# Third stage's weight conversions on a 22-unit step through the second stage

## The chip, the cores and the metric

The kernel runs on one core of a Trainium2 chip. A core has five engines with queues of their own: TensorE (PE in the profile, its weight loads PEld) for matmuls, VectorE (DVE), ScalarE (ACT), GpSimd (POOL) and SyncE (SP), which here only issues DMAs. The metric is the device time of one execution in microseconds. Before the change it was 1767.12 us, the median of three runs (1766.98 to 1773.9).

## The reference

Three stages on 4608 tokens of 512 numbers: attention over pooled keys and values, a mixture of eight experts of which each token takes two, and a dense layer pair with a curved activation.

```python
x = _attn_ref(q, k, v)                              # 8 x 8 heads x 576 x 64, reshaped to (4608, 512)
# second stage: 8 experts, w1 (8, 512, 1024), w2 (8, 1024, 512), top two per token
noisy = x @ w_gate + np.log1p(np.exp(x @ w_noise)) * noise
for e in range(8):
    h = np.maximum(x[mask] @ w1[e], 0.0)
    out[mask] += top2_w[mask, k, None] * (h @ w2[e])
# third stage: w_in (512, 2048), w_out (2048, 512)
h = x @ w_in
return (h - np.tanh(h)) @ w_out
```

## The kernel before

Every matmul of the second and third stage is made of three 16-bit ones: each operand is split into a high and a low half, and high x high, high x low and low x high are added in fp32. So weights have to be prepared before use: their largest absolute value gives a power of two as scale, ScalarE writes the high half, VectorE the low half.

The second stage goes expert by expert. An expert has 1216 token slots in three groups of 512, 384 and 320, and a group has eight units, one per 128 columns of the hidden layer: 24 units an expert, numbered 0 to 23 here, 192 in all. A unit is: the first layer for this unit (`L1`, 12 matmuls, lines 356 to 358, result `ph`), its relu in two halves `hT` (ScalarE line 360, VectorE line 361), now and then one block of 128 tokens of the next group, gathered by GpSimd (line 315), split into halves `xp` (lines 341, 342) and transposed by a DMA (line 343), and then the second layer of the unit two before (`L2`, lines 378 to 385, result `py`). When a group is done `Y` scales its results and stores them (lines 402 to 410) and takes their squares. There are two buffers of `ph`, four of `py`, five of `hT`, one of `xp`.

Other work rides along, put into units by a table of jobs written at lines 552 to 590: `at((e, u), f)` puts `f` behind the matmuls of unit u of expert e, and jobs of a unit run in the order in which they were put there. The order of each engine's instructions follows from it, nothing is scheduled later. The jobs are:

- The next expert's weights, c1 (w1) and c2 (w2): `load` into `stage`, `amax` (VectorE, line 127, four pieces), `fin1` (a TensorE transpose of the column of maxima, line 170, and a reduction, line 173), `fin2` (a matmul that spreads the maximum, line 183, and the scale, lines 101 to 103), `split` (lines 154 and 159, four pieces, into `pair`).
- The third stage's weights, eight conversions `Conv`, 0 to 3 for the four quarters of w_in, 4 to 7 for those of w_out. Each is loaded in eight pieces of 256 KB into the two buffers of `raw`, and each piece is turned from the given form of numbers into fp32 in `qf` by six VectorE instructions (`conv`, lines 239 to 244). Behind the eighth come `stat` (VectorE's maximum, line 248, and for w_in seven GpSimd instructions for the sum of squares, lines 252 to 255), `fin1`, `fin2`, `norm` (a matmul over the sums, line 271), `split` (lines 290, 291, into `wi` or `wo`), and for w_in `combos` (four VectorE instructions, lines 277 to 280) and the splits of these, stored to `ws_d`.

Units 0 to 7 of expert 0 share the engines with the end of the router: it still has to make the lists `idx` of tokens per expert (lines 1442 to 1517), and is dealt out in steps: `run_jobs` gives it a turn, `gate(4)`, of up to four steps after every job, and there are further turns in a unit. At the end of unit 7's first layer it is run to its end, and the first gathers from `x_d` follow; their tokens are transposed on TensorE (line 333).

```python
def run_jobs(key, between):
    for f, a in jobs.pop(key, []):
        f(*a)
        between()
...
            run_jobs((groups[i][0], KF * groups[i][1] + f), lambda: u < KF and gate(4))
```

Of the kernel before, what the change touches and what calls it, by code (L numbers as in the profile page):

```python
# [10 lines left out]
F32 = mybir.dt.float32  # L11
F16 = mybir.dt.float16
BF16 = mybir.dt.bfloat16
I32 = mybir.dt.int32
# [23 lines left out]
def kernel(ctx, tc, q, k, v, w_gate, w_noise, noise, w1, w2, w_in, w_out, out):  # L38
# [54 lines left out]
    with ExitStack() as st:  # L93
        moe(nc, tc, st, V, z)
# [81 lines left out]
def both(g):  # L176
    for _ in g:
        pass
# [8 lines left out]
def moe(nc, tc, st, V, z):  # L187
    w_in, w_out, hold, idx, ps, W, gate, sums = (V[n] for n in ("w_in", "w_out", "hold", "idx", "ps", "W", "gate", "ws_d"))
    N, E, DM, FF, F2, NT = (V[n] for n in ("N", "E", "DM", "FF", "F2", "NT"))
    identf, ones1, onec, x_d, y_d, wi, wo, cin, wn2, outc = (  # L190
        V[n] for n in ("identf", "ones1", "onec", "x_d", "y_d", "wi", "wo", "cin", "wn2", "outc"))
    wk = st.enter_context(tc.tile_pool(name="m_wk", bufs=2))
# [3 lines left out]
    KD, KF = DM // 128, FF // 128  # L196
# [7 lines left out]
    for e in range(E):  # L204
        c = 0
# [5 lines left out]
    class Conv:  # L211
# [34 lines left out]
        def stat(self):  # L246
            self.m = wk.tile([128, 1], F32, name="cq")
            nc.vector.tensor_reduce(self.m, self.f, axis=AX.XY, op=OP.max, apply_absolute_value=True)
            if self.which == 0:
                s = self.s = wk.tile([128, 512], F32, name="qs", bufs=1)  # L250
                s2 = wk.tile([128, 512], F32, name="qs2", bufs=1)
                nc.gpsimd.tensor_mul(s, self.f[:, 0], self.f[:, 0])
                for m in range(1, 4):
                    nc.gpsimd.tensor_mul(s2, self.f[:, m], self.f[:, m])
                    nc.gpsimd.tensor_add(s, s, s2)
# [41 lines left out]
    def at(key, f, *a):  # L297
        jobs.setdefault(key, []).append((f, a))
# [255 lines left out]
    for e in range(E):  # L554
        if e + 1 < E:
            c1, c2 = PR[e + 1, 1], PR[e + 1, 2]
            d = 4 if e == 0 else 0
            for c in range(4):
                at((e, d + c), c1.load, [c])
            at((e, 7 + d), lambda c=c1: both(c.fin1()))  # L560
            at((e, 8 + d), lambda c=c1: both(c.fin2()))
            for c in range(4):
                at((e, 3 + d + c), c1.amax, c)
                at((e, (12 if d else 10) + c), c1.split, c)
                at((e, 18 + c // 2), c2.amax, c)
                at((e, 22 + c // 2), c2.split, c)
            at((e, 15 if d else 13), c2.load)
            at((e, 20), lambda c=c2: both(c.fin1()))
            at((e, 21), lambda c=c2: both(c.fin2()))
        cv = Conv(e // 4, e % 4)  # L570
        for j in range(8):
            u = (0, 1, 2, 3, 8, 10, 11, 13)[j] if e == 0 else j + 3 if e < 5 else (j + 2 if j < 6 else j + 4) if e + 1 < E else (j + 4 if j < 5 else j + 6)
            if j < 2 and e == 0:
                cv.load(j)
            elif j < 2:
                at((e, j + 2 * (e + 1 == E)), cv.load, j)
            at((e, u), cv.conv, j)
            if j + 2 < 8:
                at((e, u), cv.load, j + 2)
        at((e, 14), cv.stat)  # L580
        at((e, 15), cv.fin1)
        at((e, 16), cv.fin2)
        at((e, 16), cv.norm)
        for j in range(4):
            at((e, 20 + j // 2), cv.split, j)
            if cv.which == 0:
                if j == 0:
                    at((e + 1, 0), cv.combos)
                at((e + 1, 1 + j // 2), cv.split, j, True)

    def clear():
        zero = wk.tile([128, DM], F32, name="ys", bufs=3)
# [8 lines left out]
    for u in range(len(units) + LAG):  # L601
        if u < len(units):
            i, f = units[u]
# [3 lines left out]
            n = -(-groups[i + 1][3] // 128) if i + 1 < len(groups) else 0  # L607
# [1152 lines left out]
```

## Time and profile before

| | us |
|---|---|
| median of three runs | 1767.12 |
| profiled execution, whole | 1768.31 |
| its span in the profile | 1766.5 |
| TensorE busy in the span | 1724.0 |
| VectorE busy | 1285.0 |
| ScalarE busy | 922.6 |
| GpSimd busy | 277.0 |

The second stage lies from about 217 to 1045 us of the span. A timeline row gives the start, the length, the engine and line, the operation with what it writes and reads, its form and count, and in brackets the idle time of the engine before it with what ended it. Rows of neighbouring instructions of one kind may be merged, and lengths of matmuls overlap, since they are pipelined. A windows row gives a stretch, its length, each engine's busy time in it, and then the granted clock of TensorE as a share of 2.4 GHz.

### The profile page before, as it was taken

Reading aid. Unit: us, or ns where it says so; the run is one execution under the profiler, and the core shown is the slowest. Engines: PE = TensorE matmul, PEld = TensorE weight load, DVE = VectorE, ACT = ScalarE, POOL = GpSimd, SP = SyncE. Lnnn points to the kernel's source line nnn. Section 1 sums busy time; section 2 is a strip of 40 time slices with the busy share of each in tenths; the row PEclk is TensorE's granted clock in tenths of the full one; section 3 lists DMA queues with packets and bytes.
Section 4 is the critical chain, followed back from the end, with each engine's and each line's share of the span. In section 5 each row is a group of like instructions: output and inputs, shape, how many; then the busy total and the mean of one; then the engine's idle time right before and its main releaser. Section 6 shows DMA issues by size and latency. Waiting matters only on the chain. (4 is left out here: it accounts for less than half of the span.)

```text
span 1766.5 us, 28298 instructions
## 1 busy us (share of the span) xinstructions
PE 1724.0 (98%) x10456; PEld 1037.9 (59%) x10456; DVE 1285.0 (73%) x2566; ACT 922.6 (52%) x2229; POOL 277.0 (16%) x291
## 2 busy tenths in 40 slices
PE   8988899999999999999999999999999999999998
PEld 6988744455454545545454544666666666666664
DVE  7899867766667676666564558688787879788765
ACT  6887624434343443424243356466575757666554
POOL 3343113022030301101010111012020101110000
PEclk9999999999999999999999999999999999999999
DMA  9967334644755565554553435242231414131100
GB/s 249 274 174 199 97 101 133 164 129 138 223 135 158 139 146 149 140 134 123 155 144 81 125 94 147 55 90 69 46 93 39 88 27 96 36 79 53 33 25 26
DMA packets 264127, 203.44 MB, mean 115 GB/s; under 512 B 188129, under 2 KB 208609, under 8 KB 263969
## 3 DMA queue, kind: packets, MB, share of 16 engines
q1 hardware_dynamic: 251808, 162.16, 34.8%
q0 software_dynamic: 11904, 38.81, 8.5%
q8 instruction: 87, 1.43, 0.3%
q14 instruction: 72, 0.58, 0.1%
q10 hardware_dynamic: 256, 0.46, 0.1%
HBM read 121.82 MB, written 45.74 MB: 95 GB/s over the span
## 5 line engine op out<-in xcount | busy, mean ns | idle before, releaser
L360 ACT ACTIVATE hT<-ph 128x512 f16<-128x512 f32 (+2 forms) x192 | 96.9, 505 | 438.8 <-PE ph L358 427.9
L356 PE MATMUL ph<-xTp,pair 128*128 128x384 f16 (+2 forms) x736 | 245.5, 334 | 1.1 <-PEq L456 0.6
L357 PE MATMUL ph<-xTp,pair 128*128 128x384 f16 (+2 forms) x736 | 245.0, 333 | 1.6 <-issue 1.6
L358 PE MATMUL ph<-xTp,pair 128*128 128x384 f16 (+2 forms) x736 | 245.1, 333 | 0.0
L361 DVE SCALAR_TENSOR_TENSOR hT<-ph,hT 128x512 f16<-128x512 f32 (+2 forms) x192 | 110.8, 577 | 179.5 <-ACT hT L360 176.1
L1047 PE MATMUL py<-wo,gT 128*128 128x512 f16 x576 | 218.4, 379 | 1.0 <-issue 1.0
L1045 PE MATMUL py<-wo,gT 128*128 128x512 f16 x576 | 218.4, 379 | 0.1
L379 PE MATMUL py<-pair,hT 128*128 128x512 f16 x576 | 218.4, 379 | 0.0
L1046 PE MATMUL py<-wo,gT 128*128 128x512 f16 x576 | 218.4, 379 | 0.0
L380 PE MATMUL py<-pair,hT 128*128 128x512 f16 x576 | 218.4, 379 | 0.0
L378 PE MATMUL py<-pair,hT 128*128 128x512 f16 x576 | 218.4, 379 | 0.0
L904 PEld LDWEIGHTS <-wi 128*128 128x128 f16 x1536 | 150.2, 98 | 59.0 <-DMA y<-yp 0.9
L315 POOL DMA_INDIRECT xg<-x_d,idx x75 | 78.7, 1050 | 667.2 <-DVE xp L342 510.3
L718 POOL DMA_INDIRECT y<-y_d,ridx x64 | 78.8, 1232 | 519.0 <-DVE y L729 240.7
L356 PEld LDWEIGHTS <-pair 128*128 128x128 f16 x768 | 75.3, 98 | 76.3 <-issue 15.8
L357 PEld LDWEIGHTS <-pair 128*128 128x128 f16 x768 | 75.4, 98 | 58.7 <-issue 2.9
L358 PEld LDWEIGHTS <-pair 128*128 128x128 f16 x768 | 75.4, 98 | 57.0 <-issue 1.1
L1004 ACT ACTIVATE th<-th,bias 128x512 f32<-128x512 f32 x144 | 102.5, 711 | 3.3 <-DVE th L1002 1.6
L1005 DVE SCALAR_TENSOR_TENSOR th<-th,t 128x512 f32<-128x512 f32 x144 | 98.8, 686 | 1.4 <-ACT th L1004 1.4
L1001 DVE SCALAR_TENSOR_TENSOR t<-hb,cinf,hs 128x512 f32<-128x512 f32 x64 | 48.0, 750 | 70.8 <-ACT hs L1000 68.7
L994 DVE TENSOR_TENSOR gT<-th,gT 128x512 f16<-128x512 f32 x144 | 98.9, 687 | 0.2 <-ACT gT L993 0.2
L1047 PEld LDWEIGHTS <-gT 128*128 128x128 f16 x576 | 56.3, 98 | 69.3 <-issue 1.5
(317 smaller groups left out, 3429.3 us busy)
## 6 DMA issues: line engine op xcount, KB each, us to landing
stage<-in_moe_w SPq DMA_DIRECT2D x64, 512.0 KB
y_d<-ys SPq DMA_DIRECT2D x82, 256.0 KB
x_d<-xr SPq DMA_DIRECT2D x36, 256.0 KB
out<-o SPq DMA_DIRECT2D x36, 256.0 KB
qt<-in_q SPq DMA_DIRECT2D x32, 256.0 KB
raw<-in_moe_w_in SPq DMA_DIRECT2D x32, 256.0 KB
raw<-in_moe_w_out SPq DMA_DIRECT2D x32, 256.0 KB
kt<-in_k SPq DMA_DIRECT2D x7, 768.0 KB
```

The source lines that it names most:

```text
L356: nc.tensor.matmul(p[:, :nt], w[:, 0, m, s], x[:, 0, m, :nt], start=(m == 0), stop=False)
L357: nc.tensor.matmul(p[:, :nt], w[:, 0, m, s], x[:, 1, m, :nt], start=False, stop=False)
L358: nc.tensor.matmul(p[:, :nt], w[:, 1, m, s], x[:, 0, m, :nt], start=False, stop=(m == KD - 1))
L361: stt(h[:, 1, :nt], p[:, :nt], 0.0, h[:, 0, :nt], op0=OP.max, op1=OP.subtract)
L378: nc.tensor.matmul(p, h[:, 0, s], w[:, 0, f], start=(f == 0), stop=False)
L379: nc.tensor.matmul(p, h[:, 0, s], w[:, 1, f], start=False, stop=False)
L380: nc.tensor.matmul(p, h[:, 1, s], w[:, 0, f], start=False, stop=(f == KF - 1))
L904: nc.tensor.matmul(p, w[:, a, m], y[:, c, b, m], start=(start and m + x == 0), stop=(m == 1 and x == 2), skip_group_check=True)
L1004: nc.scalar.activation(q, q, AF.Square, bias=bias[:, 2:3], scale=SP5)
L1045: nc.tensor.matmul(p, g[:, 0, s], wo[:, 0, f], start=(f == 0), stop=False)
L1046: nc.tensor.matmul(p, g[:, 0, s], wo[:, 1, f], start=False, stop=False)
L1047: nc.tensor.matmul(p, g[:, 1, s], wo[:, 0, f], start=False, stop=(f == KF - 1))
```

## The change

The conversions are no longer one per expert. Conversion n (0 to 6) begins to load at unit 14 + 22n of the 192 and converts in the eight units of 17 + 22n to 29 + 22n that have most room by a table of VectorE work per unit (`room`); the maximum follows one unit after the last piece, then the first spread, the scale, and one unit behind it the sum and the splits. Conversion 7 stays in expert 7. By this the eight pieces of conversion 0 lie in units 20 and 21 of expert 0 and 0 to 5 of expert 1; of conversion 3 in units 11 to 21 of expert 3; of conversions 4, 5 and 6 up to units 21, 16 and 16 of experts 4, 5 and 6. The sums of squares are made in buffers of `raw` in place of `qs` and `qs2`. `fin1` and `fin2` of the next expert's w1 come one unit later in experts 1 to 6 (units 8 and 9).

```diff
@@ class Conv, stat
-                s = self.s = wk.tile([128, 512], F32, name="qs", bufs=1)
-                s2 = wk.tile([128, 512], F32, name="qs2", bufs=1)
+                s = self.s = wk.tile([128, 512], I32, name="raw", bufs=2).bitcast(F32)
+                s2 = wk.tile([128, 512], I32, name="raw", bufs=2).bitcast(F32)
@@ jobs
-            at((e, 7 + d), lambda c=c1: both(c.fin1()))
-            at((e, 8 + d), lambda c=c1: both(c.fin2()))
+            at((e, 7 + d + (e > 0)), lambda c=c1: both(c.fin1()))
+            at((e, 8 + d + (e > 0)), lambda c=c1: both(c.fin2()))
...
-        cv = Conv(e // 4, e % 4)
-        for j in range(8):
-            u = (0, 1, 2, 3, 8, 10, 11, 13)[j] if e == 0 else j + 3 if e < 5 else (j + 2 if j < 6 else j + 4) if e + 1 < E else (j + 4 if j < 5 else j + 6)
...
-            at((e, u), cv.conv, j)
...
-        at((e, 14), cv.stat)
-        at((e, 15), cv.fin1)
-        at((e, 16), cv.fin2)
-        at((e, 16), cv.norm)
-        for j in range(4):
-            at((e, 20 + j // 2), cv.split, j)
-            if cv.which == 0:
-                if j == 0:
-                    at((e + 1, 0), cv.combos)
-                at((e + 1, 1 + j // 2), cv.split, j, True)
+    size = [3 * KF * e + d for e in range(E) for d in range(3 * KF)]
+    room = [(5100, 3850, 3200)[u % (3 * KF) // KF] - (690, 580, 490)[u % (3 * KF) // KF] for u in size]
...
+    for u in range(0, 13):
+        room[u] = 0
+    step = 22
+    last = 3 * KF * (E - 1)
...
+    for n in range(8):
+        cv = Conv(n // 4, n % 4)
+        u0 = 16 + step * n if n < 7 else last + 4
+        us = sorted(sorted(range(u0 + 1, u0 + 14), key=lambda u: -room[u])[:8]) if n < 7 else             [last + d for d in (4, 5, 6, 7, 8, 11, 12, 13)]
+        for j, u in enumerate(us):
+            room[u] -= 1950
+            if j < 2:
+                unit(u0 - 2 + j, cv.load, j)
+            unit(u, cv.conv, j)
             if j + 2 < 8:
+                unit(u, cv.load, j + 2)
+        u0 = us[-1] - 13 if n < 7 else last
+        unit(u0 + 14, cv.stat)
+        unit(u0 + 15, cv.fin1)
+        unit(u0 + 16, cv.fin2)
+        unit(u0 + 17, cv.norm)
         for j in range(4):
+            unit((u0 + 17 if n < 7 else last + 20) + j // 2, cv.split, j)
+        if cv.which == 0:
+            unit(u0 + 19, cv.combos)
+            for j in range(4):
+                unit(u0 + 20 + j // 2, cv.split, j, True)
```

On TensorE, at the end of the router in expert 0, `l_row` and `l_col` are the tables from which the last lists come, `ph` is the first layer's result. Before, the last of its matmuls and what stands around them:

```order
L380 MATMUL py<-pair_2883,hT 128x512
L1513 LDWEIGHTS l_row
L1513 MATMUL pt<-l_col,l_row 128x160
...
L356 LDWEIGHTS pair_1481
L356 MATMUL ph<-x0T,pair_1481 128x512
```

The same place now (lines behind the table of jobs are 24 higher):

```order
L358 MATMUL ph<-x0T,pair_1481 128x512
L1537 LDWEIGHTS l_row
L1537 MATMUL pt<-l_col,l_row 128x160
...
L378 LDWEIGHTS hT
L378 MATMUL py<-pair_2883,hT 128x512
```

The matmuls stood between a second layer and the first layer of unit 7, and stand behind that first layer now.

On VectorE at the same place, `idx` being the lists and `hT` the relu's low half, before:

```order
L1508 TENSOR_TENSOR l_row<-slot,g_row 128x512
L361 SCALAR_TENSOR_TENSOR hT<-ph,hT 128x512
L1516 TENSOR_TENSOR idx<-pt,idx 128x8x10
L1517 TENSOR_TENSOR idx<-pt,idx 128x8x10
...
L1734 TENSOR_TENSOR coef<-dd,coef 128x36
L361 SCALAR_TENSOR_TENSOR hT<-ph,hT 128x512
L336 TENSOR_TENSOR xTp<-pt,xTp 128x4x128 x3
```

and now:

```order
L1532 TENSOR_TENSOR l_row<-slot,g_row 128x512
L361 SCALAR_TENSOR_TENSOR hT<-ph,hT 128x512
L1540 TENSOR_TENSOR idx<-pt,idx 128x8x10
L1541 TENSOR_TENSOR idx<-pt,idx 128x8x10
...
L1758 TENSOR_TENSOR coef<-dd,coef 128x36
L336 TENSOR_TENSOR xTp<-pt,xTp 128x4x128 x3
```

The hT of unit 7 stood behind the lists and the work on `coef`; now it is the one ahead of `idx`.

On VectorE in units 22 and 23 of expert 3, where `pair` is the next expert's w2 and `cq` the conversion's maximum, before:

```order
L361 SCALAR_TENSOR_TENSOR hT<-ph,hT 128x320
L159 SCALAR_TENSOR_TENSOR pair_6892<-stage,wsc,pair_6892 128x1024 x2
L361 SCALAR_TENSOR_TENSOR hT<-ph,hT 128x320
L159 SCALAR_TENSOR_TENSOR pair_6892<-stage,wsc,pair_6892 128x1024 x2
L361 SCALAR_TENSOR_TENSOR hT<-ph,hT 128x512
```

and now:

```order
L361 SCALAR_TENSOR_TENSOR hT<-ph,hT 128x320
L159 SCALAR_TENSOR_TENSOR pair_6859<-stage,wsc,pair_6859 128x1024 x2
L248 TENSOR_REDUCE cq<-qf 128x1
L361 SCALAR_TENSOR_TENSOR hT<-ph,hT 128x320
L159 SCALAR_TENSOR_TENSOR pair_6859<-stage,wsc,pair_6859 128x1024 x2
L173 TENSOR_REDUCE cx<-pt 1x1
L361 SCALAR_TENSOR_TENSOR hT<-ph,hT 128x512
```

The maximum over the whole quarter and the reduction that follows its transpose came in, behind the splits that were put into these units first.

## Rows read from the trace of the kernel before

**Rows 1.** Windows view by expert: stretch, length; engine busy (count); clock, DMA share, GB/s

```profile
431.80:535.40 103.60, 102.23 (x540) 50.96 (x539) 69.58 (x137) 41.60 (x76) 19.17 (x17) 1.00 0.62 171
...
738.20:839.20 101.00, 101.00 (x539) 50.98 (x538) 63.68 (x127) 38.84 (x73) 9.50 (x10) 1.00 0.52 137
```

**Rows 2.** Timeline, TensorE: start, length, line, operation, out<-in, form, count [idle <-releaser]

```profile
242.13 0.19 PE L1469 MATMUL pt<-mb,before 128*128 128x64 bf16 x1 [1.15 <-DVE mb L1465]
...
278.96 0.27 PE L170 MATMUL pt<-identf,cm 128*1 128x128 f32 x1 [1.78 <-DVE cm L130]
...
296.31 0.27 PE L170 MATMUL pt<-identf,cq 128*1 128x128 f32 x1 [1.10 <-DVE cq L248]
...
300.44 0.38 PE L183 MATMUL pt<-cx,onec 1*128 1x1 f32 x2 [0.29 <-DVE cx L173]
301.36 1.02 PE L271 MATMUL pt<-qs,onec 128*1 128x512 f32 x2 [0.55 <-POOL qs L255]
...
469.77 0.27 PE L170 MATMUL pt<-identf,cm 128*1 128x128 f32 x1 [0.85 <-DVE cm L130]
470.56 0.32 PE L356 MATMUL ph<-xTp,pair 128*128 128x384 f16 x1 [0.52 <-DMA xTp<-xp]
```

**Rows 3.** Timeline, VectorE, expert 0, unit 9.

```profile
274.31 0.75 DVE L408 TENSOR_SCALAR ys<-py,ysc 128x512 f32<-128x512 f32 x1 [1.24 <-DMA y_d<-ys]
```

**Rows 4.** Timeline, expert 0, unit 7, four engines.

```profile
253.38 0.44 PE L1513 MATMUL pt<-l_col,l_row 128*128 128x160 f16 x4
253.66 0.38 PE L356 MATMUL ph<-x0T,pair 128*128 128x512 f16 x1
253.86 0.24 DVE L1516 TENSOR_TENSOR idx<-pt,idx 128x80 int32<-128x80 f32 x1 [1.55 <-PE pt L1513]
...
255.29 0.94 POOL L315 DMA_INDIRECT xg<-x_d,idx  x1 [53.49 <-DVE few L1724]
...
256.25 0.38 PE L378 MATMUL py<-pair,hT 128*128 128x512 f16 x1
...
257.08 0.69 DVE L361 SCALAR_TENSOR_TENSOR hT<-ph,hT 128x512 f16<-128x512 f32 x1
...
258.84 0.60 PE L333 MATMUL pt<-identf,xg 128*128 128x128 f32 x4
```

**Rows 5.** DMA view, issues of gathers: out<-in, queue, operation, count, median us to landing.

```profile
xg<-x_d,idx POOLq DMA_INDIRECT x75, 5.0
...
y<-y_d,ridx POOLq DMA_INDIRECT x64, 3.3
```

**Rows 6.** Windows view, one conversion of expert 0, VectorE alone: stretch, length, busy (count).

```profile
270.90:272.50 1.60, 1.57 (x7) 1.00 1.11 200
```

**Rows 7.** Timeline, VectorE and TensorE, expert 5, units 17 and 18.

```profile
818.71 0.30 PE L356 MATMUL ph<-xTp,pair 128*128 128x320 f16 x1
818.89 0.49 DVE L361 SCALAR_TENSOR_TENSOR hT<-ph,hT 128x320 f16<-128x320 f32 x1 [2.50 <-ACT hT L360]
```

**Rows 8.** Timeline, VectorE and TensorE, end of expert 3.

```profile
631.11 2.48 DVE L159 SCALAR_TENSOR_TENSOR pair<-stage,wsc,pair 128x1024 f16<-128x1024 f32 x2 [0.55 <-ACT pair L154]
...
634.49 0.39 PE L356 MATMUL ph<-xTp,pair 128*128 128x512 f16 x1
```

**Rows 9.** Timeline, GpSimd and VectorE, expert 0, units 13 to 16.

```profile
290.93 1.05 POOL L252 TENSOR_TENSOR qs<-qf 128x512 f32<-128x512 f32 x1
290.97 3.08 DVE L159 SCALAR_TENSOR_TENSOR pair<-stage,wsc,pair 128x1024 f16<-128x1024 f32 x1
293.98 2.27 DVE L248 TENSOR_REDUCE cq<-qf 128x1 f32<-128x2048 f32 x1
...
298.13 2.06 DVE L159 SCALAR_TENSOR_TENSOR pair<-stage,wsc,pair 128x1024 f16<-128x1024 f32 x1
```

**Rows 10.** Timeline, TensorE, and windows view around 217.

```profile
217.16 0.61 PE L356 MATMUL ph<-x0T,pair 128*128 128x512 f16 x1 [2.29 <-DVE idx L1517]
...
215.20:222.00 6.80, 4.84 (x12) 1.80 (x13) 3.41 (x11) 0.83 (x1) 0.00 (x0) 0.50 0.35 117
```

More of the change, by code (lines that the diff above doesn't have):

```diff
@@ L569, in moe @@
             at((e, 21), lambda c=c2: both(c.fin2()))
-        cv = Conv(e // 4, e % 4)
-        for j in range(8):
-            u = (0, 1, 2, 3, 8, 10, 11, 13)[j] if e == 0 else j + 3 if e < 5 else (j + 2 if j < 6 else j + 4) if e + 1 < E else (j + 4 if j < 5 else j + 6)
[L573 to L576, printed above, removed]
-            at((e, u), cv.conv, j)
-            if j + 2 < 8:
-                at((e, u), cv.load, j + 2)
@@ new lines, in moe @@
+    for e in range(E):
+        o = 3 * KF * e
+        for d, w in ((9, 1200), (17, 600), (1, 1800 * (e > 0))):
+            room[o + d] -= w
+        for d in (0, 2, 5, 8, 10, 13, 15, 17, 19, 21):
+            room[o + d] -= 690
+        for c in range(4):
+            room[o + 3 + 4 * (e == 0) + c] -= 1200
+            room[o + (12 if e == 0 else 10) + c] -= 1300
+            room[o + 18 + c // 2] -= 1200
+            room[o + 22 + c // 2] -= 1300
+    for u in range(0, 13):
+        room[u] = 0
@@ new lines, in moe, with unit @@
+    step = 22
+    last = 3 * KF * (E - 1)
+    def unit(u, f, *a):
+        at(divmod(u, 3 * KF), f, *a)
+    for n in range(8):
[7 more added lines that the diff above has]
+            unit(u, cv.conv, j)
+            if j + 2 < 8:
+                unit(u, cv.load, j + 2)
[4 more added lines that the diff above has]
+        unit(u0 + 17, cv.norm)
+        for j in range(4):
+            unit((u0 + 17 if n < 7 else last + 20) + j // 2, cv.split, j)
[3 more added lines that the diff above has]
+                unit(u0 + 20 + j // 2, cv.split, j, True)
```

## The prediction

> **What bounds the kernel now.** I read the windows view first, by expert of the second stage [rows 1]. In expert 5 TensorE is busy 101.00 of 101.00 us at a granted clock of 1.00; in expert 2 it is busy 102.23 of 103.60 us. VectorE is busy 63.68 and 69.58 us in these two, so a third of its time is free. So the stage runs at TensorE's pace, and what the change moves (VectorE instructions, their loads, GpSimd's sums) shows in the time only where TensorE waits. All of it is done as often as before. What can be won is TensorE's idle time, what can be lost is a new wait of TensorE.
>
> Then TensorE's timeline for the waits themselves [rows 2]. Seven of them lie where the change reaches: 1.15 us for the router (L1469), 1.78 us for the first maximum of expert 1's weights (L170 <- cm), 1.10, 0.29 and 0.55 us for expert 0's conversion (L170 <- cq, L183, L271), 0.85 us again for a first maximum and 0.52 us for the transposed tokens behind it, both in expert 2. That is 6.24 us, 0.35% of the time: the change cannot gain much more than this, since the other experts stand at TensorE's pace.
>
> **Expert 0, the conversion gone from units 0 to 16.** The waits of 1.10, 0.29 and 0.55 us were for its maximum, its scale and its sum, which now come an expert later, with the sum's matmul a unit behind the scale: -1.94 us. The 1.78 us stay. The step waited for sits behind an eviction that VectorE could not write before a store had landed, until 274.31 [rows 3]; what follows it up to the maximum is the chain that TensorE waited for, and no conversion stands in it (one comes behind it, one had ended before 274.31).
>
> **The router behind units 0 to 7.** After each job of these units the router gets a turn of four steps. Ten jobs (four, two, two, two) leave units 0 to 3, so the router has ten turns less, and the order shows its pieces later: the last list matmuls, which stood ahead of the first layer of unit 7, stand behind it, and on VectorE the two idx additions come behind unit 7's hT. The 1.15 us wait goes, since four conversions no longer stand ahead of mb and its matmul comes a unit later. TensorE would reach the first token transpose at 258.84 - 1.15 = 257.69 [rows 4]. Ahead of it are a second layer (256.25 to 258.84, 2.59) and the list matmuls (253.38 to 253.66, 0.28), so unit 7's first layer ends at 254.82. Its hT starts 0.83 after that (257.08 against 256.25) at 255.65, and idx 0.6 later, at 256.25. From idx to the gather 1.43 (253.86 to 255.29): 257.68. The gather's landing has no row; it lay at most 3.55 us behind its start (TensorE took the tokens at 258.84 with no idle time) and not under the 0.94 of the instruction itself. Of the medians of the gathers, 5.0 us for those of x and 3.3 for those of y [rows 5], the first is past the 3.55; I take 3.3: 260.98. TensorE idles 3.3 us there and is 260.98 - 258.84 = 2.1 us later than before, the 1.15 us counted. Bounds: -1.15 (it lands in time) to +2.4.
>
> **First maximum a unit later, experts 1 to 6.** The matmul that waited 0.85 us in expert 2 has a whole unit (two layers of 2.59) more: -0.85. In that expert 0.52 us were for a token transpose that lay in the queue behind eleven stores of zeros and, ahead of these, two stores of sums that waited for the conversion's last step. The sums now go out at units 10 and 11, so the loads and transposes of units 2 to 5 go earlier: -0.52.
>
> **The conversions' new places.** Each still has six instructions, 1.6 us of VectorE [rows 6]. In units 0 to 12 of the experts they replace each other or the combinations and splits of the conversion before, a unit has 4.2 us on average (101 over 24) and VectorE 2.9 us of work in it (69.58 over 24), and TensorE needs a unit's hT only two units later, so that 1.6 us more in one unit are made up in the next: nothing. In unit 17 of experts 2 and 3 one stands between an eviction and the hT at 818.89, ahead of which VectorE waited 2.50 us for ScalarE (the same units in expert 5 [rows 7]): 1.6 in 2.5 us: nothing. The cover is gone there if anything above 0.9 us joins it. In experts 5 and 6 the maximum stands there instead: eviction to 816.39 (818.89 - 2.50), L248 with its 2.27 [rows 9] to 818.66, against TensorE's next unit at 818.71: 0 to 0.2 us each, taken as nothing.
>
> **The maximum in unit 22 of experts 3 and 4.** Here L248 comes behind the two conversions of the second weights, and its transpose on TensorE at the end of unit 23. In expert 3 before, the two conversions ran 631.11 to 633.59, TensorE began the next expert at 634.49 [rows 8]. L248 from 633.55 for 2.27 ends at 635.82, the transpose starts at 635.9: 1.4 us idle in expert 4. In expert 3 GpSimd's seven sums start with the last conversion too, just ahead of unit 22. Beside these sums in expert 0 such a conversion took 3.08 and 2.06 us [rows 9], against 1.24 each in rows 8: 1.8 and 0.8 more. I take the mean of the two for each of the two conversions, 2.6: 4.0 us idle in expert 3. Bounds: 1.4 (no collision) to 5.0 (1.8 twice). Behind the waiting transpose stands all of expert 4's first layer; behind L248 on VectorE hT of unit 23, two more conversions and the reduction, whose readers come one to two units later, so nothing is added.
> The page "SBUF — State Buffer" of the Trainium skill, section "Who interferes with whom", has a rule for this: a VectorE instruction with two SBUF inputs and a GpSimd instruction that reads SBUF exclude each other, the later one waits until the other has ended, and a reduction never collides. The 3.08 and 2.06 us agree, and so does L248 at 2.27 beside the sums. By the rule each of the two conversions waits out one or two of GpSimd's instructions of 1.05 us, 2.1 to 4.2 us in all in place of my 2.6.
>
> **Sums in the slots of raw, not in qs.** A following conversion's first load now waits for the sum's matmul. It comes 3 units behind it or more (unit 9 and 12 of expert 1, 7 and 10, 5 and 8, 1 and 6 in the next): over 10 us, nothing. Nor do I count a gain: no row shows a wait for qs but the 0.55 us counted.
>
> **Sum.** -1.94 - 0.85 - 0.52 = -3.3; +2.1 + 4.0 + 1.4 = +7.5; together +4.2 us. The profiled execution took 1768.31 us (span 1766.5), so its like would take 1772.5. The median of the runs is 1767.12, 1.2 us below it, and so I say 1771.3 us: 0.24% slower, which counts as no change, since a measurement of this kernel cannot tell differences below about 0.5% (8.8 us).
>
> **Rivals.** (a) The new waits stay covered: the gather lands before TensorE is there, and VectorE has the maximum in time. -3.3 - 1.15: 1762.7 us. For it: the landing is not shown, and VectorE is idle for 0.55 us just ahead of the two conversions [rows 8]. Against: the hT ahead of idx and the length of L248 leave no such room.
> (b) The clock. TensorE idled 2.29 us at 217.16 [rows 10], and over 215.2 to 222 its granted clock was 0.50, the lower of its two levels (1.2 GHz of 2.4). That costs half of 6.8, 3.4 us, a time. The new waits of 3.3 and 4.0 us are longer than that one. If the clock falls at both: 1771.3 + 6.8 = 1778.1, slower by 0.6%; at one, 1774.7. It decides from the point where one of the waits exceeds what the clock bears; against it, 1.78 us of idle left the clock at 1.00 [rows 1, 2].
> The page "TensorE: Matmul & The Clock Gate" of the Trainium skill, section "HAM oscillation — how this bites in real kernels", speaks for (b): gaps in TensorE's work put the clock back to half, and every burst behind one starts slow.
> (c) The queue. Raw loads now lie in units 12 to 17 of experts 1 to 4, beside the 2 MB of the second weights, and the token transposes share their queue. A transpose that lands late cost 0.52 us in expert 2; once in each of four experts is 2.1 us: 1773.4. Against: the transposes of unit 17 have seven units until they are read.
>
> **Chances and range.** Forecast 0.65, its own range 1767.5 to 1774.0 (expert 3 between 1.4 and 5.0, expert 0 down to 0). (a) 0.17, (b) 0.11 of which 0.04 at both places, (c) 0.07. To hold 8 in 10 the range goes to the middle of (a) and past (b) at one place: 1763 to 1776. Slower by over 0.5% (above 1775.9): (b) at both, and half of its other cases with the upper bounds of expert 0 and 3, 0.08. Faster by over 0.5% (below 1758.3) would need more than all waits of rows 2: 0.03. Within 0.5%: 0.89.
>
> **What would show it.** In the profile of the changed kernel: L1469 without idle time; the first transpose of gathered tokens with 2.5 to 3.7 us of it, released by the gather; L170 <- cq with about 4 us at the end of expert 3 and 1.4 at the end of expert 4, and none elsewhere; L159 of 2 to 3 us just ahead of the former; no wait for cm in expert 2, but still 1.5 to 1.8 us at the start of expert 0's second group; expert 5 and 6 at 100.9 to 101.3 us. It is wrong if the transposes at the ends of experts 3 and 4 do not wait, if the gather's transpose does not, or if the granted clock leaves 1.00 behind 222 us.

## The result, and the profile after

The changed kernel took 1784.6 us (median of six runs, 1780.27 to 1788.62) against 1769.57 us for the kernel before on the same chip (six runs, 1766.98 to 1773.9): a ratio of 1.0084, interval 1.0063 to 1.0105. That is slower by 0.84%, where 1771.3 us and a range of 1763 to 1776 us had been forecast. The profiled execution took 1780.27 us (span 1778.4), 11.96 us more than that of before, where the sum said 4.2.

First the windows view by expert, the columns as in [rows 1]: stretch, length, the engines' busy time, then TensorE's granted clock. These are experts 1 to 4 of the changed kernel.

```profile
330.00:436.10 106.10, 102.20 (x540) 50.95 (x539) 74.39 (x148) 41.48 (x76) 18.52 (x17) 1.00 0.57 145
436.10:538.10 102.00, 102.00 (x540) 50.99 (x539) 74.58 (x149) 41.33 (x76) 19.20 (x17) 1.00 0.60 178
538.10:646.90 108.80, 103.97 (x541) 51.41 (x540) 78.59 (x150) 41.47 (x76) 28.88 (x24) 0.98 0.52 137
646.90:751.00 104.10, 102.17 (x542) 50.97 (x540) 69.06 (x136) 41.50 (x77) 10.60 (x10) 1.00 0.53 143
```

Expert 2, which idled before, is full now: 102.00 us busy of 102.00. Experts 1, 3 and 4 are not. Expert 3 has a second mark, a clock of 0.98 and 2 us more of busy time for the same matmuls (the stretch takes in the start of expert 4). The waits themselves stand in TensorE's timeline, to be held against [rows 2]; in brackets the idle time and what ended it.

```profile
262.31 0.63 PE L333 MATMUL pt<-identf,xg 128*128 128x128 f32 x4 [3.29 <-DMA xg<-x_d,idx]
282.59 0.27 PE L170 MATMUL pt<-identf,cm 128*1 128x128 f32 x1 [1.91 <-DVE cm L130]
316.28 0.27 PE L170 MATMUL pt<-identf,cm 128*1 128x128 f32 x1 [0.64 <-DVE cm L130]
412.89 0.38 PE L378 MATMUL py<-pair,hT 128*128 128x512 f16 x1 [1.93 <-ACT ys L406]
422.38 0.27 PE L170 MATMUL pt<-identf,cm 128*1 128x128 f32 x1 [1.96 <-DVE cm L130]
627.67 0.27 PE L170 MATMUL pt<-identf,cm 128*1 128x128 f32 x1 [1.14 <-DVE cm L130]
642.36 0.27 PE L170 MATMUL pt<-identf,cq 128*1 128x128 f32 x1 [3.69 <-DVE cq L248]
735.80 0.27 PE L170 MATMUL pt<-identf,cm 128*1 128x128 f32 x1 [0.65 <-DVE cm L130]
748.08 0.27 PE L170 MATMUL pt<-identf,cq 128*1 128x128 f32 x1 [1.28 <-DVE cq L248]
```

The first, seventh and ninth row are the three waits that the prediction named: 3.29, 3.69 and 1.28 us, where it said 3.3, 4.0 and 1.4. The 1.78 us of expert 0 stayed (1.91). The waits of 1.15, 1.10, 0.29, 0.55, 0.85 and 0.52 us are gone. What it did not have are the rows at 316.28, 412.89, 422.38, 627.67 and 735.80. One of them has a forerunner in the kernel before that neither the prediction nor [rows 2] lists, in expert 1:

```profile
418.09 0.27 PE L170 MATMUL pt<-identf,cm 128*1 128x128 f32 x1 [0.50 <-DVE cm L130]
```

All five lie in the last group of an expert, where the second weights of the next one come in. In expert 1 two engines stand still there. ScalarE and VectorE, units 16 and 17:

```profile
409.04 0.29 DVE L239 TENSOR_SCALAR ca<-raw 128x256 int32<-128x256 int32 x1 [4.89 <-DMA raw<-in_moe_w_in]
411.63 0.63 ACT L341 ACTIVATE xp<-xg 128x512 f16<-128x512 f32 x1 [4.42 <-DMA xTp<-xp]
412.17 0.67 ACT L406 ACTIVATE ys<-py,ysc 128x512 f32<-128x512 f32 x1
412.90 0.74 DVE L408 TENSOR_SCALAR ys<-py,ysc 128x512 f32<-128x512 f32 x1
```

ScalarE wants to write the next tokens into `xp`, but the transpose of the ones before has not left it: there is one `xp`. VectorE wants to convert a piece of `raw` that has not landed. Behind the one stands the eviction L406, behind the other L408, TensorE needs their `py` back, and the maximum of the second weights (L127, L130) comes behind all that. SP's queue, seen as issues (start, length, line, operation, count), shows what stands ahead of both late transfers:

```profile
395.36 2.11 SPq L120 DMA_DIRECT2D stage<-in_moe_w  x4
397.57 1.20 SPq L293 DMA_DIRECT2D ws_d<-ys  x2
398.86 0.56 SPq L225 DMA_DIRECT2D raw<-in_moe_w_in  x1
401.42 2.05 SPq L343 DMA_TRANSPOSE xTp<-xp  x1
403.56 6.87 SPq L225 DMA_DIRECT2D raw<-in_moe_w_in  x2
```

The 2 MB of w2 are ahead, then two stores of sums (which the change moved here) and the raw load that VectorE waits for, then the transpose. Which of these the transpose waits for is not shown: of them only the raw load was moved in a run of its own (the second experiment below), and ScalarE still waited.

The clock is the last part. TensorE alone around the 3.69 us wait; the last three columns are clock, DMA share and GB/s:

```profile
640.00:642.30 2.30, 0.00 (x0) 1.00 0.00 0
642.30:645.00 2.70, 2.64 (x8) 0.56 0.00 0
645.00:647.00 2.00, 2.00 (x9) 0.74 0.00 0
647.00:649.00 2.00, 2.00 (x11) 1.00 0.00 0
```

The engine was idle, and when it came back it worked at the lower level (1.2 GHz) for some 3.4 us (an estimate from the two windows with a lower clock: twice 2.70 x 0.44 + 2.00 x 0.26). The first layer behind it took 4.43 us (642.47 to 646.90) instead of 2.59: 1.8 us.

### The profile page after: what moved, and what is told of

It is laid out like the page before. It is cut to its first block, busy times and chain, and to the rows that moved or that the text cites. A ratio compares the mean times of both kernels' runs of the same rounds, so it can differ in the third digit from the quotient of the medians.

```text
span 1778.4 us, 28325 instructions
## 1 busy us (share of the span) xinstructions
PE 1727.3 (97%) x10454; PEld 1041.3 (59%) x10456; DVE 1287.6 (72%) x2566; ACT 922.5 (52%) x2229; POOL 274.9 (15%) x291
```

## The experiments

Two questions: what makes the five unforeseen waits, and why the runs lie up to 8 us above the profiled one. All ratios are to the kernel before, run on the same chip; the changed kernel stands at 1.0084.

**Two buffers of xp.**

```diff
-        xp = wk.tile([128, 2, DM], F16, name="xp", bufs=1)
+        xp = wk.tile([128, 2, DM], F16, name="xp", bufs=2)
```

The rest of the edit makes room: the sum of a half block in `Y` stays in `ys` instead of `qs2`, and a scratch of expert 7 lies in `xp`.

> The changed kernel with two buffers xp instead of one (the scratch qs2 gives up its room: the half block of Y is summed in ys itself, one scratch of expert 7 lies in xp). Theory X: in experts 0, 1, 3 and 4 the transposes of gathered tokens now come behind raw loads in SP's queue, the one xp stays taken, ScalarE (L341) stands still ahead of the evictions L406, and the chain behind it is late. Then TensorE's waits of 1.93 (py <- ys L406) and 1.96 (cm) in expert 1 and of 1.14, 0.65 and 0.64 (cm) in experts 3, 4 and 0 fall to 0.5 in expert 1 and 0 to 0.2 elsewhere: 5.0 to 5.8 us less idle time, a ratio to the kernel before of 1.0084 - 0.003 = 1.005. Rival V: VectorE is simply too full in units 15 to 21, the cm waits stay within 0.3 us of what they were and only the 1.93 goes. Rival Q: the queue stays late, and the first layer waits for xTp instead, the time does not move (1.008).

Measured: 1779.78 us, ratio 1.0057 (1.0037 to 1.0077). The 1.93 us are gone, cm in experts 0, 3 and 4 fell to nothing, 0.30 and nothing, but in expert 1 the wait for cm is still there. TensorE and VectorE of this kernel:

```profile
416.33 0.27 PE L170 MATMUL pt<-identf,cm 128*1 128x128 f32 x1 [1.56 <-DVE cm L130]
...
404.23 0.30 DVE L239 TENSOR_SCALAR ca<-raw 128x256 int32<-128x256 int32 x1 [3.63 <-DMA raw<-in_moe_w_in]
```

ScalarE no longer stands, VectorE does: L408 comes behind the late `raw`. So theory X holds for three experts and for half of expert 1; rival V, a VectorE that is simply full, falls, since cm shrank in experts 0, 3 and 4 with VectorE's work unchanged.

**The first two raw loads two units earlier.**

```diff
-                unit(u0 - 2 + j, cv.load, j)
+                unit(u0 - 4 * (n < 7) - 2 * (n == 7) + j, cv.load, j)
```

> The changed kernel with the first two raw loads of conversions 0 to 6 two units earlier, which puts conversion 1's second load ahead of the 2 MB of w2 in SP's queue; xp stays single. Theory Q (the place in the queue): VectorE no longer stands 4.9 us for raw in unit 16 of expert 1, the transposes are not held up by it, and the waits of 1.93 and 1.96 us there fall to 0 and 0.5: 3.4 us, ratio 1.0065. Rival X (one xp): the transposes stay behind the 2 MB all the same, the 1.93 stays and only part of the 1.96 goes: 1.0075 to 1.0085. The waits of 0.64, 1.14 and 0.65 us (cm in experts 0, 3 and 4) lie behind single raw loads: by Q they shrink only where the second load moved.

Measured: 1784.96 us, ratio 1.0086 (1.0068 to 1.0104): nothing won. VectorE no longer waits for raw, ScalarE still waits for xp, and both of TensorE's waits stay:

```profile
411.35 0.63 ACT L341 ACTIVATE xp<-xg 128x512 f16<-128x512 f32 x1 [3.76 <-DMA xTp<-xp]
...
412.61 0.38 PE L378 MATMUL py<-pair,hT 128*128 128x512 f16 x1 [1.27 <-ACT ys L406]
422.11 0.27 PE L170 MATMUL pt<-identf,cm 128*1 128x128 f32 x1 [1.97 <-DVE cm L130]
```

The rival's outcome, and what was missing from both theories: there are two arms side by side, and the later one decides.

**Both edits.**

> The changed kernel with two xp and the loads two units earlier, without the later maximum and without the router's turns. Theory of two arms: in expert 1 ScalarE stands for the one xp and VectorE for raw that lies behind the 2 MB, and either alone makes Y late; each edit alone left the other (waits of 1.56 with two xp, of 1.27 and 1.97 with earlier loads). With both, TensorE waits neither at py nor at cm in experts 0, 1, 3 and 4 (0 to 0.3 us each); 3.3, 3.7 and 1.3 us (gather, two maxima) stay. Ratio 1.004 to 1.005, 0.001 to 0.002 below two xp alone (1.0057). Rival: the gain of the earlier loads in the full version needs the later maximum too; then 1.0055 and a wait of 1 us or more stays in expert 1 or 3.

Measured: 1775.86 us, ratio 1.0027 (1.0012 to 1.0041). In experts 0, 1 and 4 no such wait is left, in expert 3 one of 0.29 us; 3.21, 3.69 and 1.29 us stay as they should. That is lower than expected, with 1.004 just inside the interval. The earlier loads are worth nothing alone and about 0.3% once xp is double; the intervals of 1.0057 and 1.0027 overlap a little, so this size is not clear of noise, but the vanished waits in the profile are plain.

**The first maximum's spread put back.** The changed kernel with `7 + d` and `8 + d` again, run once.

> The changed kernel with the first maximum's transpose and spread put back to units 7 and 8 in experts 1 to 6. Theory: the shift alone took the 0.85 us wait for cm from expert 2; put back, TensorE waits again at unit 7 wherever VectorE is fuller than before, which by the new places (units 0 to 5 of expert 1, 0 to 3 of expert 2) is experts 1 and 2: 0.3 to 1 us each, nothing in 3 to 6. Rival: the conversions' new places took it, no such wait comes back.

Measured: 1794.99 us in its one run (1768.65 for the kernel before beside it). The theory falls: at unit 7 TensorE waits in none of experts 1 to 6. So the conversions' new places are enough to free expert 2 of its 0.85 us, and the shift was not needed for it. Of the 14.7 us by which this run lies above the profiled one of the changed kernel, some 7 go with the `xp` again, in expert 3 too this time, and the clock behind that; the rest is mostly a clock that fell behind the gathered tokens and in expert 7, about 3 us each:

```profile
626.86 0.63 ACT L341 ACTIVATE xp<-xg 128x512 f16<-128x512 f32 x1 [6.76 <-DMA xTp<-xp]
...
628.12 0.59 PE L378 MATMUL py<-pair,hT 128*128 128x512 f16 x1 [4.27 <-ACT ys L406]
```

In the other profiles with one `xp` and the new places there is no wait at this place, and the one in expert 1 lies between 0.96 us and this run's 3.38: these waits differ from run to run. One run cannot say whether the edit has a part in it.

**The spread's shift alone, in the kernel before,** run once.

> The kernel before with only the first maximum's transpose and spread one unit later in experts 1 to 6. Theory: the 0.85 us wait in expert 2 goes, the 0.52 us for the transposed tokens behind it stays or grows to 0.5 to 1.4 us (they are as late as before, and TensorE is 0.85 us sooner there), so little or nothing is won; all other waits as in the kernel before. Rival: both go, 1.4 us.

Measured: 1774.96 us in one run (1768.65 for the kernel before beside it). The 0.85 us are gone here too, and the tokens behind them are waited for longer:

```profile
474.97 0.32 PE L356 MATMUL ph<-xTp,pair 128*128 128x384 f16 x1 [1.56 <-DVE ca L241]
```

1.56 us in place of 0.85 and 0.52: the shift by itself wins nothing there. (The row names `ca`, which this matmul does not read; the bracket is inferred, and of what it reads only `xTp` is as late.) One run cannot say what the shift costs in the whole; this one was slower in places that the shift does not touch, up to the second stage and by falls of the clock in experts 0 and 7.

**The maximum of conversions 3 and 4 three units later.**

```diff
-        u0 = us[-1] - 13 if n < 7 else last
+        u0 = us[-1] - 13 + 3 * (n in (3, 4)) if n < 7 else last
```

> The changed kernel with the maximum of conversions 3 and 4 and all behind it three units later (unit 1 of the next expert in place of unit 22). Theory: the waits L170 <- cq of 3.69 us (end of expert 3) and 1.28 us (end of expert 4) go, and with the first of them the stretch at half clock behind it (1.8 us): 5 to 6.8 us less in a profile, ratio 1.0045 to 1.0055, and a smaller spread between runs if the clock fell there in the slower ones too. Rival: the maximum of 2.27 us is as late in its new place, with the seven sums beside unit 1 to 3, and TensorE waits there or at the next expert's own first maximum (1 to 3 us): ratio 1.007 to 1.009.

Measured: 1777.11 us, ratio 1.0039 (1.0028 to 1.0050). Neither wait is there, and none has come in their place at the start of experts 4 and 5. The gain is at the upper end of what was expected or above it, 5.0 us of idle time and 1.8 us of clock behind it, against 7.5 us by the medians.

**GpSimd's sums two units later, the maximum where it is.**

```diff
+        unit(u0 + 14 + 2 * (n == 3), cv.sums)
-        unit(u0 + 17, cv.norm)
+        unit(u0 + 17 + (n == 3), cv.norm)
```

> The changed kernel with GpSimd's seven sums of conversion 3 two units later than its maximum (unit 0 of expert 4) and the matmul over them one unit later. Theory: of the 3.69 us wait at the end of expert 3 the part from contention goes (two conversions at 3.86 instead of 2.48 us, and 1.9 us in the last piece's six instructions): 0.6 to 1.5 us stay, as at the end of expert 4 (1.28), and the clock does not fall behind it: 2.2 to 3.1 plus 1.8, 4 to 5 us less, ratio 1.0055 to 1.006. Rival: the place behind the two conversions is the whole cause, GpSimd being beside the point: the wait stays above 3 us, ratio 1.008.

Measured: 1779.85 us, ratio 1.0058 (1.0040 to 1.0075). Here is the contention, VectorE and GpSimd of the changed kernel, ahead of the 3.69 us wait:

```profile
632.49 1.24 DVE L239 TENSOR_SCALAR ca<-raw 128x256 int32<-128x256 int32 x1
...
634.70 1.22 DVE L244 SCALAR_TENSOR_TENSOR qf<-ca,cb 128x256 int32<-128x256 int32 x1
...
636.24 3.86 DVE L159 SCALAR_TENSOR_TENSOR pair<-stage,wsc,pair 128x1024 f16<-128x1024 f32 x2
640.03 2.27 DVE L248 TENSOR_REDUCE cq<-qf 128x1 f32<-128x2048 f32 x1
...
632.52 1.05 POOL L252 TENSOR_TENSOR raw<-qf 128x512 f32<-128x512 f32 x1
634.60 1.04 POOL L254 TENSOR_TENSOR raw<-qf 128x512 f32<-128x512 f32 x1 [1.03 <-PE ph L358]
...
637.12 1.90 POOL L254 TENSOR_TENSOR raw<-qf 128x512 f32<-128x512 f32 x1
639.10 2.13 POOL L255 TENSOR_TENSOR raw<-raw 128x512 f32<-128x512 f32 x1
```

and with the sums moved away, VectorE and TensorE:

```profile
633.86 0.28 DVE L239 TENSOR_SCALAR ca<-raw 128x256 int32<-128x256 int32 x1
...
635.12 0.42 DVE L244 SCALAR_TENSOR_TENSOR qf<-ca,cb 128x256 int32<-128x256 int32 x1
...
636.59 2.48 DVE L159 SCALAR_TENSOR_TENSOR pair<-stage,wsc,pair 128x1024 f16<-128x1024 f32 x2 [0.55 <-ACT pair L154]
638.99 2.28 DVE L248 TENSOR_REDUCE cq<-qf 128x1 f32<-128x2048 f32 x1
...
641.32 0.27 PE L170 MATMUL pt<-identf,cq 128*1 128x128 f32 x1 [1.29 <-DVE cq L248]
```

3.69 us are 1.29 of place and 2.40 of contention, and behind 1.29 us the clock stays. The two conversions L159 give 1.38 of the 2.40 (3.86 against 2.48); the rest comes from the last piece ahead of them (L239 and L244 among its six instructions), less the 0.55 us of idle time that it uses up. The reduction L248 takes the same beside GpSimd (2.27) as without it (2.28).

**Work in the waits.** 13 and 24 matmuls that nobody reads, written into a free `pt` ahead of the two long waits:

```diff
+    def fill(e, i, n, k):
+        p = psum([128, 512])
+        for _ in range(k):
+            nc.tensor.matmul(p[:, :n], W[e, 1].pair[:, 0, 0, 0:128], XTP[i][:, 0, 0, :n], start=True, stop=True)
```

> The changed kernel with matmuls nobody reads put in front of the two long waits: 13 of 128x512 (2.8 us) ahead of the first transposes of gathered tokens in expert 0, 24 of 128x320 (3.3 us) ahead of the transpose of conversion 3's maximum. The waits stay as long, TensorE only works in them. Theory C (the clock): in the three profiles so far that have the 3.69 us wait the granted clock fell behind it (1.8 us lost each time), behind the 3.3 us wait in one of three (2.8 us). Filled, the clock stays at 1.00 from 222 us to the end of expert 4: 2.5 to 4 us less in the median, ratio 1.006 to 1.007 against 1.0084, and runs that differ less. Rival: the slower runs have another cause, the ratio stays at 1.0075 to 1.009.

Measured: 1777.85 us, ratio 1.0052 (1.0034 to 1.0070). TensorE is let go as late as before, and the windows at the end of expert 3 (the matmuls lie at 639.33, the wait's rest of 0.33 us at 643.10) read:

```profile
640.00:643.00 3.00, 2.76 (x21) 1.00 0.00 0
643.00:645.70 2.70, 2.60 (x13) 1.00 0.00 0
```

No work was taken away and some was added, and the kernel is faster by 0.3%, 5 to 6 us (the intervals just overlap). Over all profiles of these kernels, the clock fell behind the 3.7 us wait in six of six, behind the 3.2 to 3.4 us wait in five of seven (not in the changed kernel's own), behind waits of 1.9 to 2.1 us inside the stage twice (1.97 and 2.03), never behind 1.3 us. For example in the kernel with the later sums, around its 3.27 us wait in expert 0:

```profile
258.00:260.40 2.40, 0.00 (x0) 0.84 0.56 135
260.40:264.00 3.60, 3.55 (x11) 0.50 0.55 154
264.00:266.00 2.00, 2.00 (x6) 0.50 0.21 86
266.00:270.00 4.00, 4.00 (x23) 0.94 0.22 62
```

What such a fall costs there can be read from the first token transpose to the next wait for cm: 21.33 us in this kernel (260.45 to 283.59, its 1.81 us of idle time taken off), 18.37 in the changed kernel, whose clock stayed (262.31 to 282.59, less 1.91): 2.96 us.

**The router's turns.** Ten empty jobs in units 0 to 3 of expert 0:

```diff
+    for u in (0, 0, 0, 0, 1, 1, 2, 2, 3, 3):
+        unit(u, lambda: None)
```

> The changed kernel with ten empty jobs in units 0 to 3 of expert 0 (four, two, two, two), so that the router gets its turns back; all else as it is. Theory: the last list matmuls stand ahead of unit 7's first layer again, the gather starts earlier, and TensorE's wait of 3.29 us at the first transposes of gathered tokens falls to 0 to 1.2 us (the kernel before had none there, but 1.15 us at the router's matmul of mb, which should not come back since no conversions stand ahead of it): 2.1 to 3.3 us less, ratio 1.0066 to 1.0072. If in the slower runs the clock fell behind that wait, another 1 to 2 us in the median: down to 1.0055. Rival: the gather's own 3.5 us are what counts and the wait stays above 2 us: 1.008.

Measured: 1778.98 us, ratio 1.0052 (1.0035 to 1.0069). No wait is left at the tokens, nor at the router:

```profile
257.13 0.60 PE L333 MATMUL pt<-identf,xg 128*128 128x128 f32 x4
```

The gain is slightly above what was expected (5.6 us by the medians against 3.3 us of idle time), which fits a clock that in most runs fell with the wait; only profiled runs show it.

**The three edits together** (two xp, later maximum, turns).

> The three edits together on the changed kernel. If the named waits are the whole loss and are independent, 5.4 (xp) + 6.8 (maximum) + 2.7 (turns) = 14.9 us go against the median of 1784.6: 1769.7, ratio 1.000, and since waits of 0.3 to 1.9 us that the kernel before had in experts 0 and 2 are gone too, down to 0.998. With a ratio above 1.003 something else in the change costs time (the sums in raw, the loads' new places). The mean granted clock should be 0.995 as in the kernel before, not 0.989 to 0.992.

Measured: 1767.52 us, ratio 0.9987 (0.9972 to 1.0002), clock 0.995. So no loss shows beyond the named waits. In expert 1 cm still waits 2.62 us, by the theory of the two arms the second one.

**The three and the earlier loads.**

> The version with two xp, the later maximum and the router's turns (0.9987 in its run), now with the first two raw loads two units earlier. If the place in the queue is what is left in expert 1, its waits of 0.77, 0.40 and 2.62 us fall to 0.5 together, and the 0.59 in expert 3 to 0: 3.3 to 3.9 us less, ratio 0.9965 to 0.997, faster than the kernel before. If the raw loads only push something else (transposes, the gathers' block), 0.998 to 1.000.

Measured: 1764.78 us, ratio 0.9967 (0.9954 to 0.9980): faster than both kernels, if by less than the 0.5% that was set as clear. Experts 1, 2 and 4:

```profile
324.70:426.60 101.90, 101.90 (x541) 51.06 (x540) 74.42 (x148) 41.38 (x77) 18.52 (x17) 1.00 0.57 151
426.60:528.60 102.00, 102.00 (x541) 50.99 (x540) 74.56 (x149) 41.32 (x77) 19.19 (x17) 1.00 0.62 179
...
630.80:732.80 102.00, 102.00 (x541) 50.99 (x540) 70.30 (x136) 41.24 (x77) 17.75 (x17) 1.00 0.55 146
```

From the second group of expert 0 to the end of expert 6 no wait above 0.25 us is left but the 1.77 us behind the store [rows 3].

## Why the prediction was wrong

By its own steps, in the profiled execution (us; a gain is negative):

| step | forecast | measured |
|---|---|---|
| expert 0's conversion | -1.94 | -1.94 |
| router and gather | +2.1 | -1.15 + 3.29 = +2.14 |
| expert 2, both waits | -1.37 | -1.37 |
| end of expert 3 | +4.0 | +3.69 |
| end of expert 4 | +1.4 | +1.28 |
| new places: expert 1 | 0 | 1.93 + (1.96 - 0.50) = +3.39 |
| new places: cm in experts 0, 3, 4 | 0 | 0.64 + 1.14 + 0.65 = +2.43 |
| clock behind the 3.69 us | 0 (rival b) | 4.43 - 2.59 = +1.84 |
| sum | +4.2 | +11.5 |

All of these lie in experts 0 to 4. The profiled runs differ by 11.96 us, but not all of that is the change: some 1.4 us had arisen by 222 us, since the granted clock was 0.50 from 113.6 to 120.4 us, in the first stage, where it was 1.00 in the kernel before. The change does not touch that stage, and in some profiles of the same kernel with another edit (two xp, earlier loads, later sums) this fall is missing. Behind expert 6 the changed kernel takes back 1.1 us.

- **Right:** the five steps that were worked out as chains of instructions, each within 0.3 us. The router's turns and the maximum behind the two conversions were the true costs that the order showed, and the runs with turns and with the later maximum took them away. The gather's chain held link by link, though the 3.3 us to its landing was a choice and not a row (TensorE took the tokens 3.46 us behind the gather's start, 258.85 to 262.31). The maximum in experts 5 and 6 cost nothing here; it cost 0.76 us in expert 5 of the kernel with turns and 1.22 in expert 6 of the one with earlier loads alone.
- **Right by luck: the size of the contention,** 2.40 us measured, 2.6 taken. The prediction put all of it on the two conversions; they lost 1.4 (3.86 against 2.48), and the piece ahead of them, which it had at nothing, made up the rest. The rule of the Trainium skill ("SBUF — State Buffer", "Who interferes with whom") was worked out, as an estimate, to 2.1 to 4.2 for the two conversions; the trace lies below that. That the Trainium skill counts tensor_scalar there among those that can take the shared port agrees with L239 (1.24 us against 0.28).
- **Wrong: the term of nothing for "The conversions' new places", and rival (c) with it.** The step compared VectorE's time with VectorE's room. It took `raw` as landed, which in unit 16 of expert 1 it was not, for 4.89 us. And rival (c) was put aside because "the transposes of unit 17 have seven units until they are read". That counts the reader of `xTp`; the transpose also sets free the only `xp`, and ScalarE, which evicts `py`, stands in front of that one unit later. This made +5.8 us, and the prediction's bounds for the step held none of it. Three runs settle it: xp alone, loads alone, both.
- **Wrong: the clock as a rival of its own, at 0.11.** Its places were right, its size too large (1.84 us behind the 3.69 us wait, 2.96 behind the other where it fell, instead of 3.4), and it was a follower of the two waits that the forecast itself had: behind 3.69 us it fell each time. It should have been a term. The measure that the prediction took for it, 2.29 us with a fall and 1.78 without, was misread. These are the rows ahead of that wait, in the kernel before and in the changed one:

```profile
214.00 0.87 PE L1513 MATMUL pt<-l_col,l_row 128*128 128x160 f16 x10 [1.94 <-DVE l_row L1508]
215.85 1.44 PE L1537 MATMUL pt<-l_col,l_row 128*128 128x160 f16 x10 [1.93 <-DVE l_row L1532]
```

In the kernel before the wait of 2.29 us ran from 214.87 to 217.16, and the clock was at 0.50 already from 215.2 on [rows 10]. In the changed kernel it was 0.51 over 215.85 to 222.70, so that it fell behind the wait of 1.93 us, with one of 1.72 still to come. So the kernel before did not show that 1.8 to 2.3 us is where a fall begins; the runs show only how often it came behind each wait. The Trainium skill's rule that gaps put the clock back ("TensorE: Matmul & The Clock Gate", "HAM oscillation — how this bites in real kernels") agrees with the 3.69 us every time, with the 3.3 us five times in seven.

- **The median above the profile.** Its profiled run was the fastest of six. In the other five the mean granted clock is 0.989 to 0.991 against 0.992; at half speed 0.001 of 1780 us is 3.6 us long and loses 1.8, so by this estimate 2 to 5 us of the 3 to 8 between these runs and the profiled one are clock, in whatever stage. The rest would fit the xp waits, which differ from run to run; no trace of those five runs shows it. The kernel before gave 1769.57 us here against 1767.12, 2.5 us more.
- **A cause was not the one named, behind a right number:** expert 2's 0.85 us went although the spread's shift was put back, so the new places suffice for it; in the kernel before the shift alone took it away too, but the tokens' wait behind it grew.

## What to carry to other kernels

When a transfer is moved, ask two things of every other transfer behind it in the queue: who reads what it brings, and who wants the buffer that it empties; with one buffer the second is due much sooner. Where two engines can each make the same buffer late, taking one away can show little or nothing until the other is gone, so an edit that wins nothing alone is not yet refuted. And a wait that is long enough for the clock to fall has a second price in the work behind it, to be added to the forecast and not set beside it.

## What the runs showed of the hardware

A new wait does not cost the same each time: behind waits of 3.2 to 3.4 us TensorE's clock fell in five profiles of seven, behind 1.9 to 2.1 us inside the stage in two profiles, and matmuls with no use in the place of the two long waits made the kernel 5 to 6 us faster. Beside GpSimd's sums not only the two-input conversion L159 grew (1.24 to 1.93 us each) but VectorE's one-input L239 as well (0.28 to 1.24), and GpSimd's own L254 from 1.04 to 1.90 us; the reduction did not (2.27 against 2.28).
